# The second product of a Mamba-2 and GELU kernel with the weights stationary: 256 tokens move at a time, and VectorE turns the sums

## The chip, the cores and the metric

The kernel runs on one core of a Trainium2 chip. The metric is the device time of one execution in microseconds, and a kernel's time is the median over several executions. All matrix products are in fp32. TensorE (PE in the profile) multiplies, VectorE (DVE), ScalarE (ACT) and GpSimd (POOL) work on elements, and SyncE (SP) issues nearly all transfers.

## What is computed

Two layers follow each other. The first is a chunked state-space recurrence over 4 batches, 8 heads, 768 positions, head size 32 and state size 16. Its output, 3072 tokens of 256 values, goes into a feed-forward layer:

```python
def _moe_ref(x, w_in, w_out):            # x: 3072 x 256, w_in: 256 x 2048, w_out: 2048 x 256
    h = x @ w_in
    g = h * (1.0 / (1.0 + np.exp(-1.702 * h)))
    return (g @ w_out).astype(np.float32)
```

The change lies in `g @ w_out` and in how its result leaves the core.

## The kernel before

**Tiling.** The 3072 tokens are cut into six groups of 512 (`NG = 6`, `g` = 0 to 5), each of four chunks of 128. The feed-forward width of 2048 is cut into 16 tiles of 128, taken in pairs `j` = 0 to 7. Group 0 does both products plainly (`hidden`, L777, and `project_all`, L893). Groups 1 to 5 use a Strassen-Winograd scheme with seven block products in place of eight, for the first product (`first`, L837) and for the second (`product`, L936).

**The first product.** For each pair `j`, `first` issues seven matmuls (steps named 1, 6, 7, 4, 5, 2, 3 in the order string) of 256 moving columns into two PSUM banks X and Y, ScalarE copies X out between them (L863), VectorE adds (steps D and 3, `plus`, L983), and Silu follows on ScalarE (steps S and T). The result is the tile `gT[g, j]`, one of six buffers of the tag "gT".

**The second product.** `mix_g` (L929) makes VectorE combine the blocks of `gT` into `mg` (L826 to L828); `mix_w` does the same once with the weights. `product(g, j, (i,))` then adds one of the seven terms for pair `j` into its accumulator `acc`. An activation block `h` of 128 x 256 (256 tokens) is stationary, in two halves of 128 tokens, and the weight block `w` of 128 x 128 moves. So a product is two matmuls of 128 moving columns (L964), and the accumulator has tokens along the partitions. An fp32 matmul of the program stands in the profile as two MATMUL and two LDWEIGHTS records.

**Combining.** When the last pair of group `g` is done, `combine(g)` (L993) takes the seven accumulators through ScalarE (two of them, `u`, L975) and VectorE (`scaled`, L987, and `plus`) into a tile `c`, which is in a buffer of the tag "gT" too, and two transfers of 256 KB bring it to the output (`store`, L884, L887). `by_k` and the `rearrange` with `split` only give the tiles a view by halves of 128 tokens. The last group has its own ending, `end` (L1007).

**Order.** The order of work on each engine is that of the program text (`in_order`, L21). It is written out in strings. In the steady part of a group, `steady(j)` (L1200) alternates the matmuls of the first product for pairs `j` and `j - 1` with the seven products P of pair `j - 4`; M is `mix_g(g, j - 2)`. The products of the last pairs of a group (6 and 7) are issued among the first steps of the next group (L1255, L1269), and `combine(g - 1)` follows at C. Loads for later groups are issued on SP at the group's start (`load(p)`, `spread(p)`, L1250) and at `refill`.

**The start.** While the first transfers are under way, `keep_busy(10)` (L414, L1067) issues ten matmuls of 64 moving columns whose result nobody reads. After them come the masks of the first chunk (L505) and its decay terms (L511).

The two lines that issue a product are these:

```python
                nc.tensor.matmul(out=o[k] if type(o) is list else o[:, cols],
                                 lhsT=h[:, cols], rhs=w,
```

Of the kernel before, what the change touches and what calls it, by code (L numbers as in the profile page):

```python
# [8 lines left out]
FP32 = mybir.dt.float32  # L9
# [7 lines left out]
P = 128  # L17
TG = 512
# [17 lines left out]
def kernel(  # L36
# [31 lines left out]
    nc = tc.nc  # L68
# [7 lines left out]
    DM, DF = moe_w_in.shape[0], moe_w_in.shape[1] // 2  # L76
# [4 lines left out]
    NF = DF // P  # L81
    NG = T // TG
# [3 lines left out]
    R = 4  # L86
    Q = NH // R
    H = P // 2
# [10 lines left out]
    ffn = ctx.enter_context(tc.tile_pool(name="ffn", bufs=2))  # L99
# [314 lines left out]
    def keep_busy(n):  # L414

        t = bank("busy")
        for i in range(n):
            nc.tensor.matmul(out=t[:, :H], lhsT=ones, rhs=ones[:, :H],
                             start=True, stop=True, skip_group_check=True)

    def decay_heads(p, r, ab):
# [346 lines left out]
    gT = {}  # L768
# [115 lines left out]
    def store(g, half, ob):  # L884
        r0 = g * TG + half * HT
        o = out[r0:r0 + HT, :]
        nc.sync.dma_start(out=o.rearrange("(k p) d -> p k d", p=P) if len(ob.shape) == 3 else  # L887
                          o.rearrange("(k p) (c d) -> p k c d", p=P, c=2), in_=ob)

    def out_tile(g, half):  # L890
        return ffn.tile([P, 2, DM], FP32, tag="ob", name=f"ob{g}_{half}", bufs=2)
# [37 lines left out]
    def mix_g(g, j):  # L929
        t = mixed_g[g, j] = ffn.tile([P, 4, HT], FP32, tag="mg", name=f"mg{g}_{j}", bufs=3)  # L930
        mix(t, gT[g, j].rearrange("p i (t e) -> p i t e", t=2))
# [4 lines left out]
    def product(g, j, only=ORDER, ks=range(2)):  # L936
        if j == 0 and g not in acc:
            if g < NG - 1:
                a = area(f"acc{g}").rearrange("p r (t e) -> p (r t) e", t=2)
                acc[g] = [a[:, i] for i in range(7)], a  # L940
            else:

                areas.close()
                last = ctx.enter_context(
                    tc.tile_pool(name="last", bufs=1, space=bass.MemoryType.PSUM))
                tiles = [last.tile([P, 2, HT], FP32, name=f"acc{g}_{i}") for i in range(4)]
                acc[g] = [tiles[i // 2][:, i % 2] for i in range(7)], tiles

                acc[g][0][5] = [tiles[2][:, 1, :P], tiles[3][:, 1, :P]]
        B = gT[g, j].rearrange("p i (t e) -> p i t e", t=2)  # L950
        T = mixed_g[g, j]
        A, S = w_out[:, 2 * j:2 * j + 2], mixed_w[j]

        terms = ((A[:, 0, :P], B[:, 0, 0]), (A[:, 1, :P], B[:, 1, 0]), (S[:, 1], T[:, 2]),
                 (S[:, 0], T[:, 0]), (S[:, 2], T[:, 1]), (S[:, 3], B[:, 1, 1]),
                 (A[:, 1, P:], T[:, 3]))

        begins = ((0, 0), (2, 0), (5, 0), (6, 0) if g < NG - 1 else (5, 1))
        for i in only:
            w, h = terms[i]  # L960
            for k in ks:
                cols = slice(k * P, (k + 1) * P)
                o = acc[g][0][i]
                nc.tensor.matmul(out=o[k] if type(o) is list else o[:, cols],  # L964
                                 lhsT=h[:, cols], rhs=w,
                                 start=(j == 0 and (i, k) in begins),
                                 stop=(j == NF // 2 - 1), skip_group_check=True)

    def copies(g):
        u = ffn.tile([P, 4, HT], FP32, tag="gT", name=f"u{g}", bufs=6)  # L970

        c = ffn.tile([P, 2, 2, DM], FP32, tag="gT", name=f"c{g}", bufs=6)

        if g < NG - 1:
            nc.scalar.activation(u[:, 0:4:3], acc[g][1][:, 0:4:3], AF.Copy,  # L975
                                 scale=1.0 / GELU_SCALE)
        else:
            nc.scalar.activation(u[:, 0], acc[g][0][0], AF.Copy, scale=1.0 / GELU_SCALE)
            nc.scalar.activation(u[:, 3], acc[g][0][3], AF.Copy, scale=1.0 / GELU_SCALE)
        return u, c.rearrange("p t k (c e) -> p c t k e", c=2)  # L980

    def plus(o, v, w):
        nc.vector.tensor_tensor(out=o, in0=v, in1=w, op=ALU.add)  # L983

    def scaled(o, v, w):

        nc.vector.scalar_tensor_tensor(out=o, in0=v, scalar=1.0 / GELU_SCALE, in1=w,  # L987
                                       op0=ALU.mult, op1=ALU.add)

    def by_k(t):  # L990
        return t.rearrange("p (k e) -> p k e", k=2)

    def combine(g):  # L993


        u, c = copies(g)
        a = acc[g][1]
        scaled(u[:, 2], a[:, 2], u[:, 0])
        scaled(u[:, 1:3], a[:, 3:5], u[:, 2:3].to_broadcast([P, 2, HT]))
        scaled(c[:, 1, 0], by_k(a[:, 6]), by_k(u[:, 2]))  # L1000
        split = "p t (k e) -> p t k e"
        scaled(c[:, 0], a[:, 1:6:4].rearrange(split, k=2), u[:, 0:2].rearrange(split, k=2))
        plus(c[:, 1, 1], by_k(u[:, 2]), by_k(u[:, 3]))
        for t in range(2):
            store(g, t, c[:, :, t].rearrange("p c k e -> p k c e"))

    def end(g, j0):  # L1007

# [55 lines left out]
    def differ_of(p, rs):  # L1064
        differ(p, [(r, ab[p, r]) for r in rs])

    keep_busy(10)  # L1067
    ab0 = area("ab0")
    for r in range(R):
        ab[0, r] = ab0[:, r, :2 * Q * H]  # L1070
# [112 lines left out]
    def run(g, steps, products=(), **do):  # L1183


        products = iter(products)
        for step in steps.split():
            if step == "P":
                product(*next(products))
            elif step in do:  # L1190
                do[step]()
            else:
                j, i = step.split(".")
                first(g, int(j), i)
        assert next(products, None) is None

    def seven(g, j):
        return [(g, j, (i,)) for i in ORDER]

    def steady(j):  # L1200
        return "{1}.1 {0}.S P {0}.4 P {1}.6 P {0}.3 P {1}.7 {0}.T P {1}.5 P {1}.2 P {1}.D M".format(
            j - 1, j)

    def closing(k):
        return f"P {k}.S P {k}.4 P P {k}.3 {k}.T P P P"
# [40 lines left out]
    for g in range(2, NG):  # L1246
        n, p = (g + 1) * PG, (g + 2) * PG
        more, most = g + 1 < NG, g + 2 < NG
        rows = [b for b in range(NB) if most and (g + 2) * CG <= b * NC < (g + 3) * CG]
        if most:  # L1250
            load(p)
            spread(p)
            for b in rows:
                spread_rows(b)
        run(g, "0.1 P P 0.6 P P 0.7 P 0.5 P 0.2 P 0.D", seven(g - 1, 6))  # L1255
        def turn_third():
            if g == 2:
                turn_blocks(3)

        def start_third():  # L1260
            if g == 2:
                for k in n, n + 1:
                    since_start(k)

        def mask_third(k):
            if g == 2:
                mask_blocks(k)

        run(g, "1.1 t 0.S P 0.4 P P 1.6 u P 0.3 b 0.T v P 1.5 P 1.7 1.2 P 1.D C", seven(g - 1, 7),  # L1269
            C=lambda: combine(g - 1), t=turn_third, b=start_third, u=lambda: mask_third(n),  # L1270
            v=lambda: mask_third(n + 1))
        def along():
            for r in rows:
                clip_rows(r)
                decay_rows(r)

        def refill():
            if most:
                load(p + 1)
                spread(p + 1)  # L1280

        if more:

            run(g, "2.1 1.S 1.4 1.3 2.6 2.5 2.2 2.7 1.T s 2.D 2.S w 3.1 2.4 2.3 3.6 M0 3.5 3.2 3.7 2.T y "
                "refill 3.D along 4.1 4.5 4.2 3.4 P P 4.6 P 3.S P 3.3 3.T M1 4.7 P P P 4.D M2",
                seven(g, 0), s=lambda: score((n, n + 1)), w=lambda: (weigh(n), weigh(n + 1)),
                y=lambda: finish((n, n + 1)), refill=refill, along=along,
                M0=lambda: mix_g(g, 0), M1=lambda: mix_g(g, 1), M2=lambda: mix_g(g, 2))
            if most:
                decay(p)  # L1290
        else:
            run(g, "2.1 1.S 1.4 1.3 2.6 2.5 2.2 2.7 1.T 2.D M0 3.1 3.5 2.S 2.4 3.6 2.3 3.2 3.7 2.T 3.D M1",
                M0=lambda: mix_g(g, 0), M1=lambda: mix_g(g, 1))
        for j in range(5 if more else 4, NF // 2):
            run(g, steady(j), seven(g, j - 4), M=lambda: mix_g(g, j - 2))
            if most and j == 6:
                decay(p + 1)
            if most and j == 7:
                turn_blocks(g + 2)
        k = NF // 2 - 1  # L1300
        run(g, closing(k), seven(g, 4))
        if not more:
            for j in range(k - 1, k + 1):
                mix_g(g, j)
            break
        mix_g(g, 6)

        run(g, "P P A P P P P P", seven(g, 5), A=lambda: ahead(g + 1, p if most else None))
        mix_g(g, 7)
# [33 lines left out]
```

## Time and profile before

| | |
|---|---|
| median of 7 executions | 357.42 us (356.81 to 361.24) |
| the profiled execution | 359.39 us |
| its span, from the first to the last instruction | 357.4 us |
| TensorE matmul busy | 348.0 us, 3884 records |
| VectorE busy | 250.6 us, 479 instructions |
| ScalarE busy | 147.6 us |
| products (L964), all forms | 1120 matmul records |
| VectorE's transposes of 128x512 (L582) | 1.08 to 1.10 us each, 8 of them |
| DMA packets | 73055, 58552 of them under 512 B |

The span is the distance from the first instruction to the last on the core; the execution's own time is about 2 us longer. TensorE's durations are from the issue of a matmul to its modelled end, so neighbouring matmuls overlap in the records, and how fast they follow each other is read from the distance of their starts.

### The profile page before, as it was taken

To read this page: it belongs to the slowest core of one execution; us is meant where nothing else is said; L and a number is where in the kernel's file an instruction comes from. 1 tells how busy PE (TensorE), PEld (TensorE's weight loads), DVE (VectorE), ACT (ScalarE), POOL (GpSimd) and SP (SyncE) were. 2 spreads that over 40 slices of the span, in tenths; PEclk is the share of its full clock that TensorE was granted. 3 is DMA by queue.
4 is the path that set the end of the run, shared out by engine and by line. 5 is a ranking of instruction groups with operands and counts; after the bars stand their busy time and mean duration, and the time that the engine had idled before them with its cause. 6 is when DMAs were issued, how large, how long until landed. Compare 5 with 4: busy or idle time off the path is not lost.

```text
span 357.4 us, 9055 instructions
## 1 busy us (share of the span) xinstructions
PE 348.0 (97%) x3884; PEld 300.4 (84%) x3884; DVE 250.6 (70%) x479; ACT 147.6 (41%) x329; POOL 12.4 (3%) x40
## 2 busy tenths in 40 slices
PE   8989899999999999989999999999999999999996
PEld 7653458886789999879999889999889999989996
DVE  5697998999678999677598367588374444365363
ACT  3686766003353322734432554423454331453320
POOL 6210000100000100000000000000000000000000
PEclk9999999999999999999999999999999999999999
DMA  5897799553672000666005136000010000010001
GB/s 121 146 316 227 164 210 236 104 88 93 131 128 53 2 0 2 100 167 105 2 9 103 23 99 97 0 2 2 1 62 2 2 0 3 0 60 2 0 2 59
DMA packets 73055, 26.10 MB, mean 73 GB/s; under 512 B 58552, under 2 KB 66616, under 8 KB 73016
## 3 DMA queue, kind: packets, MB, share of 16 engines
q1 hardware_dynamic: 72184, 25.14, 32.1%
q8 instruction: 30, 0.49, 0.6%
q10 hardware_dynamic: 832, 0.39, 0.4%
q14 instruction: 9, 0.07, 0.1%
HBM read 22.28 MB, written 3.24 MB: 71 GB/s over the span
## 4 chain that ended last, share of the span: by engine, by line
PE 87%; SPq 4%; DMA 3%; DVE 3%; issue 1%; ACT 0%; DVEq 0%
PE acc L964 35%; PE X L858 18%; PE Y L868 14%; PE o L900 8%; PE h L783 6%; DMA bits<-in_moe_w_in_dram 3%; SPq L140 2%; PE y L742 2%; PE cb L626 2%; PE y L730 1%; SPq L166 1%; PE A L657 1%; DMA az<-in_a_dram 1%; DVE p L205 0%; SPq L253 0%
## 5 line engine op out<-in xcount | busy, mean ns | idle before, releaser
L964 PEld LDWEIGHTS acc<-mw,mg 128*128 128x128 f32 x480 | 67.1, 191 | 4.0
L964 PE MATMUL acc<-mw,mg 128*128 128x128 f32 x480 | 68.9, 275 | 0.0
L863 ACT ACTIVATE ac<-X 128x256 f32<-128x256 f32 x76 | 29.1, 382 | 83.7 <-PE X L858 83.3
L983 DVE TENSOR_TENSOR gT<-Y,ac 128x512 f32<-128x512 f32 x38 | 26.2, 690 | 42.0 <-PE Y L868 34.1
L835 ACT ACTIVATE gT<-gT 128x512 f32<-128x512 f32 (+1 forms) x76 | 39.3, 519 | 32.3 <-DVE gT L983 31.9
L964 PEld LDWEIGHTS acc<-w_out,gT 128*128 128x128 f32 x320 | 44.1, 191 | 2.6
L858 PE MATMUL X<-my,mi 128*128 128x256 f32 x152 | 45.3, 381 | 0.0
L964 PE MATMUL acc<-w_out,gT 128*128 128x128 f32 x320 | 45.3, 275 | 0.0
L983 DVE TENSOR_TENSOR gT<-Y,b 128x256 f32<-128x256 f32 x38 | 15.9, 420 | 35.1 <-PE Y L868 35.1
L783 PE MATMUL h<-yT,w_in 128*128 128x512 f32 x72 | 32.0, 596 | 1.4 <-DVE w_in L211 1.4
L900 PE MATMUL o<-w_out,gT 128*128 128x256 f32 x128 | 28.5, 381 | 0.0
L783 PEld LDWEIGHTS h<-yT,w_in 128*128 128x128 f32 x72 | 13.4, 190 | 17.9 <-issue 14.3
L826 DVE TENSOR_TENSOR mg<-gT 128x512 f32<-128x512 f32 x40 | 27.3, 681 | 0.0
L900 PEld LDWEIGHTS o<-w_out,gT 128*128 128x128 f32 x128 | 24.0, 190 | 3.4 <-issue 0.2
L858 PEld LDWEIGHTS X<-my,mi 128*128 128x128 f32 x152 | 24.7, 191 | 1.4
L964 PEld LDWEIGHTS acc<-mw,gT 128*128 128x128 f32 x160 | 23.1, 191 | 1.8
L964 PE MATMUL acc<-mw,gT 128*128 128x128 f32 x160 | 24.3, 276 | 0.0
L964 PE MATMUL acc<-w_out,mg 128*128 128x128 f32 x160 | 24.0, 275 | 0.0
L964 PEld LDWEIGHTS acc<-w_out,mg 128*128 128x128 f32 x160 | 22.8, 191 | 1.2
L863 ACT ACTIVATE b<-X 128x256 f32<-128x256 f32 x38 | 14.6, 383 | 21.5 <-PE X L858 21.1
L858 PE MATMUL X<-yT,w_in 128*128 128x256 f32 x76 | 23.3, 391 | 0.0
L868 PE MATMUL Y<-yT,mi 128*128 128x256 f32 x76 | 22.9, 383 | 0.3 <-DVE gT L983 0.3
(143 smaller groups left out, 502.1 us busy)
## 6 DMA issues: line engine op xcount, KB each, us to landing
a<-scratch SPq DMA_DIRECT2D x18, 256.0 KB, 6.0
bits<-in_moe_w_out_dram SPq DMA_DIRECT2D x4, 1024.0 KB, 7.5
x<-in_x_dram SPq DMA_DIRECT2D x24, 128.0 KB, 2.9
out_dram<-c SPq DMA_DIRECT2D x9, 256.0 KB, 3.9
bits<-in_moe_w_in_dram SPq DMA_DIRECT2D x4, 512.0 KB, 6.1
bits<-in_moe_w_in_dram SPq DMA_DIRECT2D x2, 1024.0 KB
b<-in_B_dram SPq DMA_DIRECT2D x24, 64.0 KB, 3.0
zB<-in_B_dram SPq DMA_DIRECT2D x36, 32.0 KB, 1.9
```

What stands on the lines that cost most here:

```text
L140: nc.sync.dma_start(out=dst[p][:, k], in_=src[b, :, sl, :].rearrange("h s d -> s h d"))
L626: nc.tensor.matmul(out=s["cb"][side, r, k].rearrange("p (q i) -> p q i", q=Q), lhsT=BT[rows, k, side], rhs=CT[rows, k, :, side], start=Tru ...
L742: nc.tensor.matmul(out=y[i][D * q:D * q + D, t, 2 * n + k], lhsT=rx[p][side, k, h], rhs=L[side, k, h // Q, h % Q], start=begin(i, t, (q,)) ...
L783: nc.tensor.matmul(out=h, lhsT=w_in[:, k, f * P:(f + 1) * P], rhs=yT[g][:, k], start=(k == 0), stop=(k == NK - 1))
L826: nc.vector.tensor_tensor(out=t[:, 0:2], in0=B[:, :, 1], in1=B[:, 0], op=ALU.subtract)
L835: nc.scalar.activation(o, i, AF.Silu, scale=GELU_SCALE)
L858: nc.tensor.matmul(out=s["X"], lhsT=lhsT, rhs=rhs, start=i == "1", stop=i == "4", skip_group_check=True)
L863: nc.scalar.activation(copy, s["X"], AF.Copy)
L868: nc.tensor.matmul(out=o, lhsT=lhsT, rhs=rhs, start=s.pop("new", False), stop=i != "5", skip_group_check=True)
L900: nc.tensor.matmul(out=o[k // 2][:, k % 2], lhsT=gT[g, f // 2][:, f % 2, k * P:(k + 1) * P], rhs=w_out[:, f], start=(f == 0 and k % 2 == 0 ...
L964: nc.tensor.matmul(out=o[k] if type(o) is list else o[:, cols], lhsT=h[:, cols], rhs=w, start=(j == 0 and (i, k) in begins), stop=(j == NF ...
L983: nc.vector.tensor_tensor(out=o, in0=v, in1=w, op=ALU.add)
```

## The change

Three things are altered.

1. For groups 1 to 4, `product` makes the weight block stationary and lets the activation block move. One matmul of 256 columns takes the place of two of 128. In group 1, pairs 0 to 5, it is still two matmuls of 128 columns each, with the same weights. The accumulator then has output features along the partitions and tokens along the columns. Group 5 is as before.
2. `combine` leaves the sums in `c` and issues no store. A new function, `turn_out`, transposes half of the sums on VectorE in blocks of 32 x 32 into an output tile, and issues four transfers of 64 KB on SP, in which each run in memory has 32 values (128 bytes). It is called twice in the next group: after the mixing of step 5 and after Silu T in step 6. Until then `c` is kept.
3. `keep_busy` issues seven matmuls of 192 columns in place of ten of 64.

```diff
-            nc.tensor.matmul(out=t[:, :H], lhsT=ones, rhs=ones[:, :H],
+            nc.tensor.matmul(out=t[:, :3 * H], lhsT=ones,
+                             rhs=ones[:, :H].unsqueeze(1).to_broadcast([P, 3, H]),
                              start=True, stop=True, skip_group_check=True)
...
-    keep_busy(10)
+    keep_busy(7)
...
             w, h = terms[i]
+            if g < NG - 1:
+                n = 2 if g == 1 and j < 6 else 1
+                for k in range(n):
+                    cols = slice(k * HT // n, (k + 1) * HT // n)
+                    nc.tensor.matmul(out=acc[g][0][i][:, cols], lhsT=w, rhs=h[:, cols],
+                                     start=(j == 0 and k == 0 and (i, 0) in begins),
+                                     stop=(j == NF // 2 - 1), skip_group_check=True)
+                continue
             for k in ks:
...
-        c = ffn.tile([P, 2, 2, DM], FP32, tag="gT", name=f"c{g}", bufs=6)
+        c = ffn.tile([P, 2, 2, HT], FP32, tag="gT", name=f"c{g}", bufs=6)
...
-        scaled(c[:, 1, 0], by_k(a[:, 6]), by_k(u[:, 2]))
-        split = "p t (k e) -> p t k e"
-        scaled(c[:, 0], a[:, 1:6:4].rearrange(split, k=2), u[:, 0:2].rearrange(split, k=2))
-        plus(c[:, 1, 1], by_k(u[:, 2]), by_k(u[:, 3]))
-        for t in range(2):
-            store(g, t, c[:, :, t].rearrange("p c k e -> p k c e"))
+        scaled(c[:, 1, 0], a[:, 6], u[:, 2])
+        scaled(c[:, 0], a[:, 1:6:4], u[:, 0:2])
+        plus(c[:, 1, 1], u[:, 2], u[:, 3])
+        sums[g] = c
+
+    sums = {}
+
+    def turn_out(g, i):
+
+        t = out_tile(g, i).rearrange("p k e -> p (k e)")
+        nc.vector.transpose(out=t, in_=sums[g][:, i].rearrange("p t e -> p (t e)"))
+        rows = out[g * TG:(g + 1) * TG].rearrange("(b j) d -> j b d", j=32)
+        for r in range(R):
+            cols = slice(i * P + 32 * r, i * P + 32 * r + 32)
+            nc.sync.dma_start(out=rows[:, :, cols],
+                              in_=t[32 * r:32 * r + 32].rearrange("p (b e) -> p b e", e=32))
...
-    def steady(j):
-        return "{1}.1 {0}.S P {0}.4 P {1}.6 P {0}.3 P {1}.7 {0}.T P {1}.5 P {1}.2 P {1}.D M".format(
-            j - 1, j)
+    def steady(j, also=""):
+        return "{1}.1 {0}.S P {0}.4 P {1}.6 P {0}.3 P {1}.7 {0}.T {2} P {1}.5 P {1}.2 P {1}.D M".format(
+            j - 1, j, also)
...
-            run(g, steady(j), seven(g, j - 4), M=lambda: mix_g(g, j - 2))
+            if j == 5:
+                do = lambda: (mix_g(g, 3), turn_out(g - 1, 0))
+            else:
+                do = lambda: mix_g(g, j - 2)
+            run(g, steady(j, "o" if j == 6 else ""), seven(g, j - 4), M=do,
+                o=lambda: turn_out(g - 1, 1))
```

More of the change, by code (lines that the diff above doesn't have):

```diff
@@ L979, in copies @@
             nc.scalar.activation(u[:, 3], acc[g][0][3], AF.Copy, scale=1.0 / GELU_SCALE)
-        return u, c.rearrange("p t k (c e) -> p c t k e", c=2)
+            c = c.rearrange("p t k (c e) -> p c t k e", c=2)
+        return u, c
     def plus(o, v, w):
```

## The prediction

> **What bounds the kernel now.** I read the busy times and the chain of waits on the page first, then the windows by stage, then the timeline of the stages that the change touches.
>
> ```profile
> PE 348.0 (97%) x3884; PEld 300.4 (84%) x3884; DVE 250.6 (70%) x479; ACT 147.6 (41%) x329; POOL 12.4 (3%) x40
> ...
> PEclk9999999999999999999999999999999999999999
> ...
> PE 87%; SPq 4%; DMA 3%; DVE 3%; issue 1%; ACT 0%; DVEq 0%
> ```
>
> TensorE is busy for 97% of the span and makes 87% of the chain, and its clock was granted in full. "Busy" alone proves little, since matmul ends are modelled, so I look for its idle time by stage (columns: stretch, length, busy time of PE, PEld, DVE, ACT, POOL).
>
> ```profile
> 0.00:36.70 36.70, 31.82 (x484) 20.53 (x484) 27.41 (x59) 23.68 (x40) 9.18 (x31) 1.00 0.78 200
> ...
> 147.00:202.30 55.30, 54.26 (x642) 50.03 (x641) 38.57 (x73) 22.27 (x55) 0.32 (x2) 1.00 0.42 78
> 202.30:256.40 54.10, 54.10 (x642) 50.04 (x641) 36.35 (x71) 22.26 (x55) 0.00 (x0) 1.00 0.17 33
> 256.40:310.00 53.60, 53.60 (x594) 49.44 (x593) 26.72 (x51) 20.41 (x51) 0.00 (x0) 1.00 0.04 12
> ```
>
> The stages that the change touches (147 to 310, groups g = 2 to 4 of the loop) have no TensorE gap but one of 1.04 us. So there the time is the number of matmuls by their start-to-start distance, and that distance is what the change alters. Two stretches of the timeline give it (start, length, count):
>
> ```profile
> 261.23 0.59 PE L858 MATMUL X<-my,w_in 128*128 128x256 f32 x2
> 261.66 0.59 PE L868 MATMUL Y<-yT,mi 128*128 128x256 f32 x2
> ...
> 263.39 0.59 PE L858 MATMUL X<-my,mi 128*128 128x256 f32 x2
> ...
> 350.25 1.50 PE L964 MATMUL acc<-w_out,mg 128*128 128x128 f32 x12
> 351.59 1.50 PE L964 MATMUL acc<-w_out,gT 128*128 128x128 f32 x12
> ```
>
> One fp32 matmul of the program is two records. With 256 columns moving, five matmuls start within 263.39 - 261.23 = 2.16 us: 0.432 us each. With 128 columns, 12 records take 351.59 - 350.25 = 1.34 us: 0.1117 us each, so a product of two matmuls (four records) 0.447 us. The mean durations on the page (275 and 381 ns) contain the pipeline's latency and must not be used for this sum: by them the gain would be 4 x 275 - 2 x 381 = 338 ns a product, over twenty times too much.
>
> [...] the trace says 447 - 432 = 15 ns, and I use the trace. [...] the trace of before shows 128-byte runs only as loads of x (128 KB landing in 2.9 us).
>
> **The change part by part.**
>
> *Wider products.* For g = 1 the blocks j < 6 stay at two matmuls of 128 columns, so only j = 6, 7 merge: 2 x 7 = 14 products. For g = 2, 3, 4 all merge: 3 x 8 x 7 = 168. Together 182. Where products alternate with the first product's matmuls the period of the two is 6.15 us / 7 = 0.8786 (steps such as 284.08 to 290.23 on the timeline), and 2 x 0.432 = 0.864 would take its place: again 0.0146 us. 182 x 0.0147 = 2.7 us, all on the path, because these stages are TensorE end to end. [...]
>
> *g = 1, j < 6 with w_out stationary.* Same columns, same number: 0. The moving tile is now the one that waits for VectorE or ScalarE; the weights are long there. 0.
>
> *Transposes.* Eight of 128x512 on VectorE. The same operation and shape stands in the trace as the block transposes of B and C: 1.08 to 1.10 us, so 8.7 us more of VectorE. They go into steps 5 and 6 of the next group. There VectorE waits for TensorE:
>
> ```profile
> 280.41 0.43 DVE L828 TENSOR_TENSOR mg<-gT,mg 128x256 f32<-128x256 f32 x1
> 282.08 0.42 DVE L983 TENSOR_TENSOR gT<-Y,b 128x256 f32<-128x256 f32 x1 [1.25 <-PE Y L868]
> 284.79 0.69 DVE L983 TENSOR_TENSOR gT<-Y,ac 128x512 f32<-128x512 f32 x1 [2.28 <-PE Y L868]
> ```
>
> The first transpose comes after the mixing of step 5 and falls in the gap of 1.25 us, the second after the Y + b sum of step 6 and falls in that of 2.28 us (2.63 in g = 2). Groups 2, 3 and 5 show the same two gaps. 1.09 fits in both. The first leaves 0.16 us, and a step of TensorE shortens by 7 x 0.0147 = 0.10, so it may be late by nothing or a tenth. Behind it on VectorE stands the sum that Silu, then the next mixing, then a product a step later wait for: over 3 us of slack. Cost 0; with the cover gone 1.09 us each.
>
> *The sums stay in their buffer longer.* They hold one of six gT buffers until step 6; the next user of that buffer is block 7, whose first write is VectorE's own, after the transposes. No wait. The combination's arithmetic has the same sizes and durations.
>
> *Stores.* Per group eight stores of 64 KB in 128-byte runs (4096 packets) in place of two of 256 KB in 512-byte runs (1024). They go from about 20% of a group to about 60%: at 173 to 178 us in place of 150.5. On SP's queue they are moved past the second pair's loads (zC, zB, b, x, a), which were behind the store and now come free a little earlier, and stay ahead of the next group's loads, whose first issue (185.79 us) waits for VectorE's block transposes anyway. At about 0.6 us an issue (loads of x: 1.15 us for two) they need 5 us of SP between 173 and 180. The DMA engines are nearly idle there. The last ones are issued some 20 us before the end. Cost 0; bound +0.5 if a load slips.
>
> *The gap of 1.04 us.* It lies in the burst of small matmuls of g = 2:
>
> ```profile
> 156.83 1.25 PE L742 MATMUL y<-L,x 64*32 64x64 f32 x104 [1.04 <-issue]
> ```
>
> Nothing that the profile shows released it, and the DMA engines were 0.99 busy just before (153 to 155.7 us) with the store of 150.51 and the loads behind it. I read it as a late instruction block. The change takes the store from there and moves the block boundaries (by 68 instructions before that point), so the gap can go (-1.04), stay, or come up at another burst (+1). The bursts of g = 3 and 4 show none, with the store beside them. I take half: -0.5.
>
> *Unread products at the start.* Ten of 64 columns become seven of 192. Twenty records took 5.53 - 1.21 = 4.3 us[...]what ends the first 36.7 us is the chain of w_in's transfer (landing at 29.13) and VectorE's 7.4 us of conversion, and TensorE stands waiting at its end:
>
> ```profile
> 36.74 3.67 PE h L783 x8
> ```
>
> There the timeline has 1.08 us of idle time, released by VectorE's w_in. Cost 0[...].
>
> Sum against the profiled execution (359.39 us, span 357.4): -2.7 - 0.5 = -3.2, a span of 354.2. That execution lies 2 us above the median of 357.42; the matmul spacing is the same in every run, so I take the difference from the median: 354.2 us.
>
> **Rivals.**
> *A. The gain is eaten (within 0.5%).* Faster TensorE in steps with a busy VectorE, or a second instruction gap of 1 us, leaves 1 us or so of the 2.7: 356.4. For it: the 1.25 us gap is nearly full[...]. Against it: pure streams of both widths stand in this trace. 0.14.
> *B. Slower: VectorE's transposes are exposed.* If the first transpose in each group does not fit its gap and its delay passes through Silu and mixing to the next product, TensorE waits up to 1.09 us for each: 8 x 1.09 = 8.7, less 2.7: 363.4. It decides for slower once more than 4.5 of the 8.7 us are exposed. For it: the place directly before a sum that frees a PSUM bank. Against it: VectorE waits for TensorE in every step, and products use mixings two steps old. 0.08.
> *C. The start shortens as well.* If the chain behind w_in is TensorE's after all, up to 0.8 us more, with the gap gone wholly: 352.9. 0.10.
> The forecast has the remaining 0.68.
>
> **How the numbers follow.** About 0.5% (1.8 us) is what a measurement of this kernel tells from no change. Forecast and C are faster: 0.78; A same: 0.14; B slower: 0.08. The range goes from C's 352.9 to a gain cut to 1.2 us, 356.2, which takes in the gap staying (354.7) and one coming anew (355.7).
>
> **What would show it.** TensorE's records fall by 2 x 182 + 6 to 3514 and VectorE's rise by 8 to 487; the steady period falls from 6.15 to 6.05 us in g = 2 to 4 and stays in g = 1 and 5; each of the three group stages is 0.8 us shorter; no TensorE wait on VectorE appears after steps 5 and 6; DMA packets rise by 4 x 3072 to about 85,300. A new TensorE wait in those steps, a period that stays at 6.15, or a start that ends elsewhere than 36.7 would make it wrong.

## The result and the profile after

The change makes the kernel faster by about 1%: the ratio of the new time to the old is 0.9905, with a 95% interval of 0.9882 to 0.9927. The medians are 354.9 us after (27 executions, 353.03 to 360.23) and 357.84 us before (64 executions, 356.45 to 363.72). Ratios here leave out executions that were disturbed, which the medians contain, so a ratio need not be the quotient of two medians. The forecast was 354.2 us.

The profiled execution of the changed kernel took 357.97 us and spans 356.0. That is only 1.4 us less than the profiled one of before and 3 us above the new median, so its parts must be read one by one. First the page: busy times, granted clock, instruction queue and the shares of the chain of waits.

```profile
PE 344.4 (97%) x3514; PEld 288.0 (81%) x3514; DVE 255.6 (72%) x487; ACT 147.8 (42%) x329; POOL 13.1 (4%) x40
...
PEclk9999999999999999989999999999999999999999
...
q8 instruction: 27, 0.44, 0.5%
...
PE 91%; SPq 2%; DMA 2%; DVE 2%; issue 1%; ACT 0%
```

The counts are those that were predicted: 3514 records on TensorE, 487 on VectorE. VectorE is busy for 5.0 us more, not 8.7. TensorE's share of the chain has risen from 87 to 91%. The 8 among the nines of the clock is new and lies in the 18th slice, that is at 151 to 160 us. The instruction queue moved 27 packets (0.44 MB) in place of 30 (0.49 MB).

The steady part, TensorE's timeline in group 2 (start, length, count):

```profile
170.83 0.59 PE L869 MATMUL Y<-yT,w_in 128*128 128x256 f32 x2
171.26 0.59 PE L966 MATMUL acc<-mg,w_out 128*128 128x256 f32 x2
171.69 0.59 PE L859 MATMUL X<-yT,w_in 128*128 128x256 f32 x2
...
176.87 0.59 PE L869 MATMUL Y<-yT,w_in 128*128 128x256 f32 x2
```

One step of seven first-product matmuls and seven products now takes 176.87 - 170.83 = 6.04 us, where it took 6.15. All fourteen lie 0.43 us apart, and none waits. The stage of group 3, from its first score matmul (L627) to that of group 4, reads:

```profile
206.01 1.20 PE L627 MATMUL cb<-CT,Bt 32*64 32x128 f32 x64
...
259.28 1.20 PE L627 MATMUL cb<-CT,Bt 32*64 32x128 f32 x64
```

That is 53.27 us against 54.20 before (205.36 to 259.56): 0.93 less for 56 products, 0.0166 us each.

The transposes, on VectorE's timeline of the same steps (the bracket is idle time before, and what ended it):

```profile
173.66 0.70 DVE L1020 STREAM_TRANSPOSE ob<-c 128x512 f32<-128x512 f32 x1
174.92 0.42 DVE L993 TENSOR_TENSOR gT<-Y,b 128x256 f32<-128x256 f32 x1 [0.55 <-PE Y L869]
175.26 0.70 DVE L1020 STREAM_TRANSPOSE ob<-c 128x512 f32<-128x512 f32 x1
...
177.57 0.69 DVE L993 TENSOR_TENSOR gT<-Y,ac 128x512 f32<-128x512 f32 x1 [1.62 <-PE Y L869]
```

Each takes 0.70 us. They sit in the two gaps, and 0.55 and 1.62 us of those are left, in which VectorE still waits for TensorE.

Then the one place where time was lost, the burst of small matmuls (L731, L743) in group 2, TensorE's timeline:

```profile
152.14 1.04 PE L731 MATMUL y<-CsT,S 32*64 32x64 f32 x56
153.11 0.81 PE L743 MATMUL y<-L,x 64*32 64x64 f32 x58
156.96 0.93 PE L743 MATMUL y<-L,x 64*32 64x64 f32 x70 [3.04 <-issue]
157.82 1.06 PE L859 MATMUL X<-yT,w_in 128*128 128x256 f32 x2
158.68 1.06 PE L869 MATMUL Y<-my,mi 128*128 128x256 f32 x2
```

The windows about it (stretch, length, busy times, granted clock, DMA share, GB/s) show what follows the gap:

```profile
156.90:158.00 1.10, 1.04 (x71) 0.95 (x71) 1.10 (x1) 0.08 (x1) 0.00 (x0) 1.00 0.69 68
158.00:160.00 2.00, 2.00 (x6) 1.53 (x6) 0.49 (x1) 1.36 (x3) 0.00 (x0) 0.50 1.07 151
160.00:162.20 2.20, 2.20 (x9) 1.81 (x8) 0.00 (x0) 0.38 (x1) 0.00 (x0) 0.68 0.42 119
```

The gap of 1.04 us has become 3.04 us, and soon after it TensorE runs at half clock: from 157.82 on the matmuls start 0.86 us apart, double the 0.43. Two us of gap and some 1.7 us of half clock, less the gain of spacing, make group 2 2.89 us longer than before. The whole difference of the two spans adds up from the starts of marked instructions: the fan matmuls of L398 start 2.17 us earlier (38.18 against 40.35), nothing changes from there to group 2 (-0.07), then +2.89 in group 2, -0.93 in group 3 and -1.04 from group 4 to the end: -1.32.

So two questions went to the chip. Does the spacing carry the whole gain? And what sets the gap and the start, which the forecast had as -0.5 and 0? A profile is of one execution, so each of these differences between two profiles can also be one between executions.

### The profile page after: what moved, and what is told of

Read it like the earlier page. It is cut to its first block, busy times and chain, and to the rows that moved or that the text cites. A ratio compares the mean times of both kernels' runs of the same rounds, so it can differ in the third digit from the quotient of the medians.

```text
span 356.0 us, 8349 instructions
## 1 busy us (share of the span) xinstructions
PE 344.4 (97%) x3514; PEld 288.0 (81%) x3514; DVE 255.6 (72%) x487; ACT 147.8 (42%) x329; POOL 13.1 (4%) x40
## 2 busy tenths in 40 slices
DMA packets 87773, 26.06 MB, mean 73 GB/s; under 512 B 75320, under 2 KB 81336, under 8 KB 87736
## 4 chain that ended last, share of the span: by engine, by line
PE 91%; SPq 2%; DMA 2%; DVE 2%; issue 1%; ACT 0%
PE acc L966 28%; PE X L859 19%; PE Y L869 14%; PE h L784 9%; PE o L901 8%; PE acc L973 7%; PE y L743 2%; SPq L140 2%; PE y L731 2%; PE cb L627 2%; DMA bits<-in_moe_w_in_dram 1%; PE A L658 1%; DMA az<-in_a_dram 1%; PE h L801 1%; DVE c L997 0%
## 5 line engine op out<-in xcount | busy, mean ns | idle before, releaser
L966 PE MATMUL acc<-mg,mw 128*128 128x256 f32 (+1 forms) x228 | 54.7, 346 | 0.0
L966 PEld LDWEIGHTS acc<-mg,mw 128*128 128x128 f32 x228 | 39.6, 190 | 4.6
L966 PE MATMUL acc<-gT,w_out 128*128 128x256 f32 (+1 forms) x152 | 35.7, 347 | 0.0
L859 PEld LDWEIGHTS X<-my,mi 128*128 128x128 f32 x152 | 27.5, 190 | 3.3
L966 PEld LDWEIGHTS acc<-gT,w_out 128*128 128x128 f32 x152 | 26.5, 192 | 3.3
L869 PE MATMUL Y<-my,mi 128*128 128x256 f32 x76 | 23.2, 387 | 0.1
L869 PE MATMUL Y<-yT,w_in 128*128 128x256 f32 x76 | 23.1, 386 | 0.0
L859 PE MATMUL X<-my,w_in 128*128 128x256 f32 x76 | 22.9, 386 | 0.0
L388 DVE TENSOR_TENSOR_SCAN L<-a,idents 128x1024 f32<-128x1024 f32 x9 | 20.5, 2283 | 0.0
```

What stands on the lines that cost most here:

```text
L388: nc.vector.tensor_tensor_scan(out=L, data0=ra[p].rearrange("p k e -> p (k e)"), data1=idents.rearrange("p h i -> p (h i)"), initial=0.0, ...
L859: nc.tensor.matmul(out=s["X"], lhsT=lhsT, rhs=rhs, start=i == "1", stop=i == "4", skip_group_check=True)
L869: nc.tensor.matmul(out=o, lhsT=lhsT, rhs=rhs, start=s.pop("new", False), stop=i != "5", skip_group_check=True)
L966: nc.tensor.matmul(out=acc[g][0][i][:, cols], lhsT=w, rhs=h[:, cols], start=(j == 0 and k == 0 and (i, 0) in begins), stop=(j == NF // 2 - ...
```

## The experiments

Each kernel was timed beside the kernel before on the same chip. "The kernel after" is the changed one, and numbers of executions stand in brackets.

### The wide products alone

The kernel after with its old unread products, `keep_busy(10)` of 64 columns:

```diff
-            nc.tensor.matmul(out=t[:, :3 * H], lhsT=ones,
-                             rhs=ones[:, :H].unsqueeze(1).to_broadcast([P, 3, H]),
+            nc.tensor.matmul(out=t[:, :H], lhsT=ones, rhs=ones[:, :H],
...
-    keep_busy(7)
+    keep_busy(10)
```

> The wide products and the turned sums alone, with the old ten unread matmuls of 64 columns. Theory S (spacing of the products carries the gain): 2.7 us below the kernel before, about 354.8, steady period 6.05 us in groups 2 to 4. Rival C (the start carries a part): less than half of the change's 3.4 us is left here, about 356.3. Rival G (the gap in the burst of small matmuls of group 2 decides): the time follows the length of that gap in the profile, anywhere from 353 to 358.

Measured: 355.58 us (13) against 359.19 (42), ratio 0.9899 [0.9862, 0.9935]. The same kernel on another chip:

> The wide products and turned sums alone, with the old unread matmuls and the loads where the change has them, on the same chip as the kernel with the late loads: ratio 0.9899 within the first interval, 2.7 us below the kernel before where the clock was full; gap at 14.72 blocks of 1 to 3.5 us.

It gave 354.29 (20) against 357.92 (25), 0.9913 [0.9888, 0.9937]. Products and turned sums carry all of the change's gain that can be measured. The number is cleanest among executions whose mean granted clock was at least 0.998: 354.06 (13) against 357.29 (17), -3.2 us; and on the first chip 355.42 (8) against 358.30 (22), -2.9 us. The forecast had -2.7 for this part.

The gap in the burst of group 2 differs widely between the two profiled executions of this one kernel. On the first chip it was 3.54 us, followed by half clock for 6.8 us, and the execution took 360.32 us:

```profile
157.92 1.36 PE L742 MATMUL y<-L,x 64*32 64x64 f32 x76 [3.54 <-issue]
```

On the second it was 0.35 us, with no half clock after it, in an execution of 353.68 us. The expectation of 1 to 3.5 us did not hold there.

### The fuller unread products alone

The kernel before with the change's unread products and nothing else:

```diff
-    keep_busy(10)
+    keep_busy(7)
```

and 192 columns in place of 64 in the function, as in the diff above read backwards.

> Only the unread products altered (seven of 192 columns), the rest as before. Theory S: within 0.4 us of the kernel before, though the clock is full some 3 us sooner, since the w_in transfer and VectorE end the first 37 us. Rival C: 1 to 2.2 us faster, with the wait of 2.1 us of VectorE on w_in gone. Rival G: instructions shift by 12, the gap of 1 us may change.

Measured: 359.78 (22) against 359.19, ratio 1.0012 [0.9984, 1.004]: no change in the median. Yet its profiled execution, at full clock, reached L398 at 38.66 us, 1.7 us earlier than that of the kernel before. The two seem not to fit together, and the last experiments come back to it.

### Wide products in all of group 1

The change leaves two matmuls of 128 columns in group 1, pairs 0 to 5. Here one replaces them too:

```diff
-                n = 2 if g == 1 and j < 6 else 1
+                n = 1
```

> The changed kernel with the exception for group 1, pairs 0 to 5, taken out: 42 more products of one matmul of 256 columns. Theory S: 42 x 0.0147 = 0.6 us faster than the changed kernel, about 354.0 or a little less. Rival G (instruction blocks arrive late in the burst of group 2): 168 instructions fewer before that burst move the block boundary, so the gap of 3 us in the changed kernel's profile goes or is much altered, and the median moves by more than 1 us either way. A rival on VectorE (TensorE runs ahead in group 1 into waits): no gain, new TensorE waits between 105 and 147 us.

Measured: 359.04 (14) against 359.19, ratio 0.9981 [0.9949, 1.0013]. 42 more wide products, worth 42 x 0.0147 = 0.6 us by the forecast's price, cost some 3 us: the gain is gone. Group 1 itself is shorter by 0.64 us, as priced (56.20 us from its first score matmul to that of group 2, in the kernel after 56.84), and no new wait of TensorE on VectorE appears in it. The loss comes later: the stage of group 3 takes 57.00 us against 53.27. TensorE's timeline of this kernel, its three long gaps in bursts:

```profile
156.37 1.36 PE L743 MATMUL y<-L,x 64*32 64x64 f32 x114 [1.54 <-issue]
...
212.71 0.30 PE L743 MATMUL y<-L,x 64*32 64x64 f32 x4 [1.78 <-issue]
...
269.15 0.46 PE L743 MATMUL y<-L,x 64*32 64x64 f32 x31 [1.38 <-issue]
```

The bursts of groups 3 and 4, which had no gap before or after the change, have one each, and behind that of group 3 the clock is at half for 3.4 us.

What shifted is the number of instructions ahead of them. An fp32 matmul of the program stands in the trace as four instructions of TensorE, two loads of weights and two matmuls. The instruction queue moved 30 packets of 16,384 bytes in the profile before and 27 in that after, beside 7817 and 7077 instructions that the trace has for TensorE (matmuls, loads of weights and semaphore instructions): one packet for about 261 (an estimate from these counts). Counted over the same instructions in units of 256, called blocks here, the gaps of this kernel stand at 13.75, 18.76 and 22.75. In every other kernel of the study that has a gap in group 2, it stands at 14.75 (after 3777 instructions, in the kernel before as in the kernel after). Each is 193 or 194 instructions past a multiple of 256, so any two gaps are whole blocks apart but for one instruction, and the place where they stand is taken as the end of a block. (The expectations use a count that comes out a little lower; there the same place is called 0.72.)

### Half of those pairs

A test of that reading. With pairs 3 to 5 merged, the count puts two block ends, 17.75 and 18.76, into the burst of group 3, and only one into that of group 4, which should not stall:

```diff
-                n = 2 if g == 1 and j < 6 else 1
+                n = 2 if g == 1 and j < 3 else 1
```

> The changed kernel with pairs 3 to 5 of group 1 merged as well (the exception kept for pairs 0 to 2): 21 products, 84 instructions fewer before the bursts, a third of a block. Counted from the gaps so far, block boundaries lie at 0.72 of a multiple of 256; the bursts of groups 2, 3, 4 then start at 13.50, 17.63 and 21.75 and are 1.44 to 1.5 blocks long, so those of groups 2 and 3 hold two boundaries. Theory G with boundaries: gaps of 1 to 2 us at the second boundary in groups 2 and 3, so 1 to 3 us slower than the changed kernel in spite of 0.3 us saved. Theory S: 0.3 us faster.

Measured: 359.23 (22) against 358.78 (75), ratio 0.9993 [0.9964, 1.0022]. Its timeline has gaps at 14.75 and 18.76 blocks, in groups 2 and 3, and none in group 4:

```profile
157.01 0.45 PE L743 MATMUL y<-L,x 64*32 64x64 f32 x28 [1.50 <-issue]
...
211.01 0.71 PE L743 MATMUL y<-L,x 64*32 64x64 f32 x46 [0.74 <-issue]
```

Where gaps can stand is thus settled by a count of instructions. Their lengths here, 2.24 us together, do not explain the whole loss of some 3 us against the kernel after. Among executions at full clock this kernel took 356.55 us (3), and the next experiment's, which has the kernel after's matmuls, 354.79 (3) on the same chip. That is 1.8 us, about what the lengths would give; the rest of the loss stays open.

The trace also has a record of each packet of the instruction queue. Together with the gaps it gives this table (times in us, positions in blocks):

| kernel, group | burst starts, position | gap, position | the block before ends | packet starts (took) | TensorE goes on | gap |
|---|---|---|---|---|---|---|
| before, g = 2 | 14.13 | 14.75 | 150.4 | 154.6 (0.98) | 156.83 | 1.04 |
| after, g = 2 | 13.86 | 14.75 | 148.9 | 154.4 (1.21) | 156.96 | 3.04 |
| merged from pair 3, g = 3 | 17.68 | 18.76 | 208.4 | 208.6 (0.93) | 211.01 | 0.74 |
| all merged, g = 3 | 17.35 | 18.76 | 209.3 | 210.0 (1.33) | 212.71 | 1.78 |
| all merged, g = 4 | 21.50 | 22.75 | 266.0 | 266.5 (1.23) | 269.15 | 1.38 |

"The block before" ends 256 instructions ahead of the gap. In each row a packet starts after that, and TensorE, which has meanwhile come to the end of the next block, goes on 1.2 to 1.5 us after the packet has been moved. The packet starts shortly after the end of the block before (0.3 to 0.7 us) in groups 3 and 4, but 4.2 and 5.5 us after it in the two rows of group 2. In the steady part, where no gap is seen, a block is 64 fp32 matmuls of 0.432 us, 28 us (an estimate from the spacing). A whole burst without a gap is 184 matmul records with their loads of weights, 368 instructions, in 2.4 us (shown below), so a block lasts about 256 / 368 x 2.4 = 1.7 us there (an estimate too), less than the 2.1 us or more that a packet and the time behind it take.

The bursts of groups 3 and 4 in the kernel after have no gap. They start at 18.01 and 22.15 blocks, a quarter of a block or more behind the ends at 17.75 and 21.75, and a packet has started ahead of each (at 207.66 us, the burst of group 3 at 210.36; at 260.35, that of group 4 at 263.62). The narrow pairs in group 1 are what puts them there.

### No transposes, other stores

The kernel after, its sums stored as they are, in four transfers right after the combination. It leaves out the transposition of the sums, so the values of groups 1 to 4 land in other places.

```diff
-        sums[g] = c
+        for t in range(2):
+            for i in range(2):
+                r0 = g * TG + t * HT
+                nc.sync.dma_start(
+                    out=out[r0:r0 + HT, i * P:(i + 1) * P].rearrange("(k p) d -> p k d", p=P),
+                    in_=c[:, i, t].rearrange("p (k e) -> p k e", k=2))
...
-                do = lambda: (mix_g(g, 3), turn_out(g - 1, 0))
+                do = lambda: mix_g(g, 3)
...
-                o=lambda: turn_out(g - 1, 1))
+                o=lambda: None)
```

> The changed kernel without the 32x32 transposes: the sums are stored as they are (features along the partitions, four stores of 128 KB in 512-byte runs right after the combination), so values land in other places of the output; only the turning and the 128-byte stores are left out. Theory S (transposes lie in VectorE's gaps): same as the changed kernel within 0.4 us where the clock was full, that is 2.7 us below the kernel before. Rival B (transposes exposed): up to 5.6 us faster than the changed kernel (8 x 0.70). Theory G (late instruction blocks): the stores are back beside the burst of group 2, so its gap is as long as in the changed kernel or longer, though TensorE's program is the same.

Measured: 357.52 (22) against 358.78, ratio 0.9903 [0.9874, 0.9932], the same as with transposes (0.9905). They and the 128-byte runs of their stores cost nothing that can be measured; the interval is 1 us wide to either side. The gap in group 2 was 0.68 us in the profiled execution, though the stores stand beside the burst again, so theory G's expectation of at least the changed kernel's 3.04 us missed.

### The loads beside the burst

What delays the packet in group 2? That group has loads of small runs (zC, zB, b) on SP's queue beside its burst, and in the kernel after the DMA engines are busy at 0.76 from 147 to 156 us, but at 0.01 and 0.02 about the bursts of groups 3 and 4. A first test holds the second pair's loads back until the burst is over, by a 32-byte transfer that reads what the burst produces and stands ahead of them on SP's queue:

```diff
+                mark = dram.tile([1, 8], FP32, name=f"mark{g}")
+                nc.sync.dma_start(out=mark, in_=yT[g + 1][0:1, 0, H:H + 8])
                 load(p + 1)
```

It was put into the kernel after, the kernel before, and the kernel of wide products alone.

> The changed kernel with the second pair's loads in groups 2 and 3 held back until the burst of small matmuls is over (a transfer of 32 bytes that reads the burst's result stands ahead of them on SP). TensorE's program is the same. Theory G with transfers as the cause [...]: the gap of 3 us in group 2 falls to under 0.5 us, no half-clock window after it, few executions above 356, median 1 to 3 us below the changed kernel's. Rival G2 (the block boundary alone, whatever the transfers): the gap stays at 1 us or more. Rival S (the gap costs nothing that the median shows): same median, 2.7 us below before.

> The kernel before with the same late loads. Theory G with transfers as the cause: its gap of 1 us in group 2 goes too, the executions above 360 become few, and the median falls by 0.5 to 2 us; the distance to the kernel with both is then again 2.7 us, the spacing of the products alone. Rival G2: nothing changes.

> The wide products and turned sums with the old ten unread matmuls, and the late loads of groups 2 and 3. Theory S plus G: 2.7 us below the kernel before where the clock was full, and fewer executions with half-clock windows than the changed kernel has, since the full clock comes later at the start and the burst's gap is under 1 us: ratio 0.987 to 0.990, faster than the changed kernel on the same chip by 0.5 to 2 us in the median. Rival (late loads are worth nothing and the start neither): the same as the changed kernel within 0.4 us.

| kernel | late loads: median | ratio to before | without: ratio |
|---|---|---|---|
| after | 357.0 (22) | 0.9931 [0.9904, 0.9958] | 0.9905 [0.9882, 0.9927] |
| before | 358.13 (22) | 0.9976 [0.9952, 1.0] | 1 |
| wide products alone | 356.42 (22) | 0.9925 [0.9897, 0.9954] | 0.9913 [0.9888, 0.9937] |

In the profiled executions the gap was 0.19 us in the kernel before (1.04 without late loads), 0.81 us in the kernel after and 2.76 us in the third. The kernel before may have gained a little, with an interval that reaches 1; in the other two nothing was gained. So the expected gaps, under 0.5 us in the kernel after and under 1 us in the third, did not come. The windows and the timeline of the third kernel show what happens there:

```profile
148.00:150.00 2.00, 2.00 (x12) 1.47 (x11) 1.93 (x5) 1.05 (x3) 0.00 (x0) 1.00 1.00 143
154.00:156.00 2.00, 2.00 (x110) 1.50 (x109) 1.93 (x4) 0.69 (x2) 0.00 (x0) 1.00 0.52 176
156.00:158.00 2.00, 0.06 (x5) 0.00 (x0) 0.59 (x2) 0.00 (x0) 0.00 (x0) 1.00 0.09 27
```

```profile
155.31 0.76 PE L742 MATMUL y<-L,x 64*32 64x64 f32 x52
158.82 0.99 PE L742 MATMUL y<-L,x 64*32 64x64 f32 x76 [2.76 <-issue]
```

The DMA engines are full at 148 and half full from 154 to 156, now with the first pair's transfers; while TensorE stands still, from 156 to 158, they are at 0.09. The packet started at 156.3, just when they had come to rest, 5.5 us after the end of the block before at 150.8. It is not short of bandwidth in the gap, it was late before.

So the first pair's transfers were held back as well: in the kernel of wide products with late loads, `spread(p)` moves from the group's start to behind the mark.

```diff
-            spread(p)
...
                 nc.sync.dma_start(out=mark, in_=yT[g + 1][0:1, 0, H:H + 8])
+                spread(p)
```

> Wide products, turned sums, the old unread matmuls, late loads of the second pair, and now the first pair's decay rows (a from scratch, 512 KB a group) held back as well until the burst of groups 2 and 3 is over. In all profiles so far TensorE resumed 1.16 to 1.5 us after the instruction packet had moved, and in group 2 that packet started 3.1 to 5.8 us after the boundary before it, against 0.2 to 0.7 where the queues were empty. Theory G with transfers as the cause: with fewer transfers ahead of it the packet starts earlier, within 3 us of the end of the cb matmuls, the gap is under 1 us and there is no half-clock window after it; few executions above 357; ratio 0.986 to 0.990, below the wide products alone on the same chip by 0.5 to 1.5 us in the median. Rival (the packet's start is set by something other than queued transfers): gap of 1 to 3 us as before, the same median.

Measured: 353.59 (only 6) against 357.92 (25), ratio 0.989 [0.9848, 0.9931]. Its profiled execution spans 350.9 us. TensorE's timeline and the windows of it:

```profile
152.00 1.04 PE L730 MATMUL y<-CsT,S 32*64 32x64 f32 x56
152.98 1.48 PE L742 MATMUL y<-L,x 64*32 64x64 f32 x128
154.39 0.70 PE L858 MATMUL X<-yT,w_in 128*128 128x256 f32 x2
```

```profile
150.00:152.00 2.00, 2.00 (x10) 1.50 (x8) 2.00 (x4) 0.72 (x2) 0.00 (x0) 1.00 0.05 13
152.00:154.00 2.00, 2.00 (x161) 1.93 (x162) 1.93 (x5) 0.69 (x2) 0.00 (x0) 1.00 0.00 0
```

The burst of 184 matmuls runs through in 2.4 us without a gap, at an empty DMA. The packet had started at 150.3, 1.9 us after the end of the block before at 148.5, as the expectation for transfers as the cause had it. Its stage of group 2 (from the first score matmul, 147.66 to 200.90) is 53.24 us, against 53.85 in the profiled wide products alone with a gap of 0.35 us. It is the lowest median of the study. The same kernel without the late loads had 354.29 on this chip, and the two intervals overlap widely, so that it beats the change is not shown. Nor is the cause of the late packet: this is one profiled execution, and without held loads the gap can be as short as 0.35 us.

### The unread products again

> The kernel before with the late loads and the new unread products; beside the earlier run of the kernel before with the late loads alone (ratio 0.9976, clock full in 18 of 22 executions) it shows what the unread products do when the burst's gap is small. If the early full clock helps: ratio under 0.9965. If it is harmful because TensorE then idles between 10 and 25 us and is put back to half clock: fewer than half of the executions with a full clock, ratio 1.000 to 1.005. If it is worth nothing: 0.9976 within the interval.

> The changed kernel once more, beside the other two on the same chip. Ratio 0.9905 within the first interval; its gap in the burst of group 2 is at 14.72 blocks again, of a length that need not be 3 us.

The kernel before with late loads and the change's unread products: 359.99 (14) against 359.66 (51), ratio 0.999 [0.9952, 1.0028]. Its clock was full in 3 of 14 executions, as the case for harm expected, but the ratio can't tell harm from no effect. The kernel after once more: 357.0 (22), 0.992 [0.989, 0.9949]. The profile of the latter shows what the median hides. This is its page's row of granted clock and two windows of the repeated kernel after:

```profile
PEclk9769999999999999999999999999999999999999
```

```profile
10.00:14.00 4.00, 2.76 (x139) 1.98 (x138) 2.12 (x5) 2.93 (x7) 1.69 (x3) 0.98 0.66 70
14.00:24.00 10.00, 9.81 (x166) 6.43 (x166) 6.16 (x14) 5.76 (x11) 1.75 (x3) 0.50 0.96 261
```

The fan matmuls of L398 in its timeline, and in that of the kernel with all late loads and the old unread products:

```profile
41.47 0.69 PE L398 MATMUL ab<-X,ones 32*64 32x256 f32 x16
...
38.18 0.69 PE L398 MATMUL ab<-X,ones 32*64 32x256 f32 x16
```

In the repeated kernel TensorE is at half clock again from 13.84 to 24.08 us, and the start ends at 41.5 us. In its first profile, where the clock stayed, L398 had started at 38.18. With the fuller unread products the full clock comes at 4.4 to 7.0 us of the span, with the old ones at 9.0 to 10.9. The first two profiles show what it is worth: seven bf16 matmuls of 256 columns start 0.109 us apart from 5.15 us on in the kernel after, where the record of the full clock begins at 4.41 us, and 0.213 us apart from 5.53 us on in the kernel before, where it begins at 8.96 (the page's row of the clock shows no loss ahead of that record). But with the new ones it is taken back in six of eight profiled executions, for one, two or three times 3.4 us between 12.8 and 27.1 us; with the old ones in none of the five whose trace has the clock. Executions with a mean clock of at least 0.998, hence without any such loss, were 31 of 166 with the new unread products and 55 of 83 with the old ones (37 of 61 beside wide products, 18 of 22 in the kernel before with late loads); the kernel before itself had 112 of 193.

L398 starts at 39.8 to 42.8 us where the clock is taken back, and at 38.18 and 38.66 in the two profiles with the new products where it stays. With the old products it starts at 38.2 to 40.5 us in six profiled executions. So the 2.17 us between the first two profiles are not shown to be the new products' work.

What makes the clock fall can be read in part. The granted clock changes only at times that lie whole multiples of 3.41 us apart (in the first profile of the kernel after it is full from 4.41 us, falls at 158.01, 45 of them later, and is full again at 161.42). In the six starts, TensorE's matmul records cover only 1.6 to 2.3 us of the 3.41 us just before the fall; in the repeated kernel after, 2.2 us from 10.43 to 13.84, which hold a wait of 1.24 us for a load of x. After the gaps in bursts it is the same: 1.05 us before the fall in the profiled kernel after. Of the stretches of 3.41 us that follow each other from the clock's first rise, every one with 2.32 us or more kept the clock, and three with 2.06 to 2.23 kept it too. So the falls follow stretches in which TensorE was idle for a third of the time or more, and where these stretches begin varies from one execution to the next. That the earlier full clock exposes the start's idle times to this is an explanation that no run tests.

## Why the prediction was right, and where its steps were not

**Wider products, -2.7: right, priced a little low.** The period fell to 6.04 us (predicted 6.05), the stage of group 3 by 0.93 (0.8), and wide products alone brought 2.9 to 3.2 us at full clock. The stages without a gap say the same: 0.21 us from group 1, 0.93 from group 3, 1.04 from group 4 on, and with another 0.93 for group 2 that makes 3.1 us (an estimate). Taking the price from start-to-start distances in the trace was the step that mattered.

**Group 1 with w_out stationary, 0: right in itself, blind to the rest.** Merging those pairs shortened group 1 by 0.64 us, as the price has it. That the narrow matmuls also keep a second block end out of the later bursts was not seen; merging them loses the whole gain.

**Transposes, 0: right, with a mis-sized term.** 0.70 us each in place of 1.09. The row of B and C it was taken from has the same shape and operation, so shape and operation alone did not give the price; the input here is contiguous, there it is strided, and no run separates that from other differences. Both transposes fit, rival B did not come, and no wait of TensorE on VectorE appeared.

**Stores, 0: right, with a wrong count.** Packets rose to 87,773, not 85,300: those under 512 B by 16,768, near the 16,384 reckoned, but those of 512 B to 2 KB fell by only 2,048, so a group's old stores had gone as 512 packets of 1 KB, not 1024 of 512 B.

**The gap, -0.5: the step that failed.** It was read as a late instruction block, which the counts and packets in the table bear out, but the reason for its going away, that the store of 150.51 no longer stands there, does not hold. The burst starts 68 instructions earlier, as reckoned (after 3544, before 3612), and the gap stayed where it was, after 3777. Without the store the loads behind it move up: the issue of zC starts 0.5 us after the stage's first score matmul (148.32 and 147.79 us), before 1.4 us after it (151.47 and 150.03). The packet came 6.6 us after that matmul, before 4.6, which makes the 2.0 us by which the gap grew. Nor is it a fixed cost: the same kernel had 3.04 us in one profiled execution and 0.58 in the other, wide products alone 3.54 and 0.35. In these profiles it was thus 0.7 us shorter to 2.5 us longer than before, with the store gone from that place in all of them. That the forecast came out within 0.7 us of the median although this term was wrong is in part luck: the products gave somewhat more than their 2.7, about as much as the wrong term had added. The ratio of 0.9905 stands for 0.0095 x 357.84 = 3.4 us, against 3.2 forecast.

**Unread products, 0: right in the median, with a loss unseen.** It was argued that the transfer of w_in and VectorE's conversion end the start. In the profile of before they do. But of the six profiled executions with the old unread products only one other has these waits of TensorE for w_in; in the remaining four TensorE runs through from 25 us on and reaches L398 at 38.2 to 39.1 us, as in the profile after. So what ends the start varies between executions, whatever the unread products. For rival C's 0.8 us, the author's estimate, speaks only that the unread products alone, at full clock, took 357.47 us (5) against 358.30 (22). Against it stands a loss that no case held, the clock being taken back in most executions.

**Still open:** what delays an instruction packet by 5.5 us in one execution and by 3.1 in the next of the same kernel, what TensorE does in the 1.2 to 1.5 us after the packet is there, and whether the stretches of low activity are all that takes the clock back near 14 us. The best start with the best loads (unread products that keep the clock, with all loads of the group held back) was not tried.

## What to carry to other kernels

Price a change of matmul width from the distance of starts in stretches without a gap, not from durations (here 0.43 us against 0.59). Count TensorE's instructions: a burst of tiny matmuls that contains the end of a block of 256, counted as here, stalled for up to 3.5 us, four times out of four when it held two ends, and a change far upstream moves them. Transfers beside such a burst are the first suspect for a late block, though that is not proven here. Unread products that reach the full clock sooner (at 4.4 to 7.0 us in place of 9.0 to 10.9) are not yet a gain: look whether the clock is kept, over many executions. And do not take a difference between two single profiles for the work of a change before a second profile of the same kernel has been seen.

## What the runs showed of the hardware

- TensorE's gaps in bursts stood 193 or 194 instructions past a multiple of 256 in every kernel of the study that had one (14.75 blocks in the kernel before, the kernel after and the wide products alone), and in the five of the table TensorE went on 1.2 to 1.5 us after the packet of 0.9 to 1.3 us had moved.
- After the idle time of 3.04 us in the kernel after, TensorE ran at half clock for 3.4 us, and after one of 1.78 us in the kernel with all pairs merged too. After one of 2.76 us in another kernel it did not: its matmuls went on 0.43 us apart.
- The granted clock changed only at multiples of 3.41 us from its first rise, and fell only after such a stretch in which TensorE's matmul records covered 0.6 to 2.3 us, the end of the program left out.
- A 128x512 fp32 transpose of VectorE took 700 to 705 ns here and 1.08 to 1.10 us in the transposes of B and C.
